# Splitting the preparation of a bias block's x into two parts in an attention and mixture-of-experts kernel

## The chip, the cores and the metric

The kernel runs on one core of one Trainium2 chip. The metric is the device time of one execution in microseconds; lower is better. Five engines work side by side, each through its own list of instructions in order, and meet through semaphores: PE (TensorE, matmuls), DVE (VectorE), ACT (ScalarE), POOL (GpSimd) and SP, which issues most DMAs.

## The reference

Attention with a learned position bias, then a dense layer pair, then a mixture of experts. The change touches the bias alone:

```python
def _attn_ref(q, k, v, w1, b1, w2):          # B, H, S, D = 4, 8, 576, 64
    scores = scale * np.matmul(q, k.transpose(0, 1, 3, 2))
    rel = (pos[:, None] - pos[None, :])
    psi_rel = np.log1p(np.abs(rel)); psi_i = np.log1p(np.maximum(pos[:, None], 1.0))
    x = (psi_rel / psi_i)[..., None]          # 576 x 576 x 1
    h = np.maximum(x @ w1 + b1, 0.0)          # w1: 1 x 32
    bias = h @ w2                             # w2: 32 x 8, one plane for each head
    scores = scores + bias.transpose(2, 0, 1)[None]
    ...                                       # softmax, times v
# then moe: (clip(h + 3, 0, 6) * h / 6) @ w_out, then moe2: 8 experts, top 1 of 8 by a gate
```

## The kernel before, in words

The whole program is written out as straight code by Python, and each engine runs its instructions in the order in which the code emits them.

The 576 query rows are cut into five chunks (`CH`): chunk 0 has 64 rows, chunks 1 to 4 have 128. The bias of a chunk is made in 9 blocks of 64 key columns, so there are 45 blocks; the text numbers them 0 to 44, and blocks 9, 18, 27 and 36 are the first of chunks 1 to 4. A block goes through these steps:

- `bias_load` gives the block its tiles of x, in turn out of five buffers (xb0 to xb3 and cv), and loads them by SP. In chunk 0 a block has one tile. In chunks 1 to 4 it has two of 128 x 1024 numbers, which this document calls its first and its second **half**.
- `bias_h` makes max(w1 x + b1, 0) in each half, one instruction per half. The table `KIND` says where: kind T on DVE out of a table (L231), kind D on DVE in place (L224), kind A on ACT in place (L221).
- `bias_mm` multiplies by w2 on PE into the PSUM tile pb (L240): the first half feeds column groups 0 and 1 of the array, the second half groups 2 and 3. Then pb is evicted to the SBUF tile bt (L246 and L249 on ACT, L253 on DVE).
- `bias_tr` transposes bt on PE into pbt (L263), and two instructions evict pbt into the bias planes: on ACT for kinds A and T (L273, L277), on DVE for kind D (L277).

In `emit`, `step_m(i)` is the first three for block i, and a lambda of `bias_tr` the last. The list `bq` orders them as m(0), m(1), t(0), m(2), t(1), m(3), ...; at a chunk's end it is m(8), t(7), t(8), m(9), m(10), t(9), and so on. `bh(i)` prepares every block up to i that is not prepared yet, and `step_m(i)` calls `bh(i + 1)` ahead of its own products. The steps are dealt out, 18 for each chunk, over the 36 places marked B in the string `ORDER0`, between the attention of the first three units (six items s for each chunk):

```python
ORDER0 = "Q0 T0 X0 B Q1 X1 B S T1 B P B B B N"
```

Q is a pair's scores (sc, L324 on PE) and the reading of them with the bias by DVE (L327); X the exponentials (L335, ACT); N the norm (L341, L342 on DVE, L344 on POOL); T the transposes of an item three steps back (pt, L362 on PE, evicted to eT by L366 on ACT and L368 on DVE); P its product with v (po, L378 and L382 on PE, evicted by L386 on ACT). pb, pbt, pt and po take their PSUM banks in turn from four (m0 to m3), so each waits until the tile four allocations before it has been evicted.

The stage with these blocks lies at about 10 to 172 us of the profiled execution. Attention of the other units follows, then the dense layers, then the experts.

Of the kernel before, what the change touches and what calls it, by code (L numbers as in the profile page):

```python
# [157 lines left out]
class Attn(Base):  # L158
# [48 lines left out]
            ts.append(x)  # L207
        return ts

    def bias_h(self, c, blk, ts):  # L210
        nc = self.nc
        r0, R = CH[c]
        kind = KIND[c][blk]
        nt = R // 64
        if kind == "T" and not self.lib[c][1]:
            lb = self.lib[c][0]
            nc.vector.tensor_scalar(lb[:, 1, :], lb[:, 0, :], self.nb1, None, op0=ALU.mult)
            self.lib[c][1] = True
        for t, x in enumerate(ts):
            if kind == "A":  # L220
                nc.scalar.activation(x, x, AF.Relu, bias=self.b1c, scale=self.w1c)  # L221
            elif kind == "D":

                nc.vector.tensor_scalar(x, x, self.w1c, self.nb1, op0=ALU.mult, op1=ALU.max)  # L224
            else:

                ncg = 4 // nt
                o = blk * 64 + t * ncg * 4 - r0 + 575
                v = self.tab[:, 0:1]
                view = bass.AP(tensor=v.tensor, offset=v.offset + o, ap=[v.ap[0], [4, ncg], [16, 4], [-1, R]])  # L230
                nc.vector.tensor_tensor(x, view, self.lib[c][0][:, 1:2, :].rearrange("p (a o) r -> p a o r", o=1).to_broadcast([P, ncg, 4, R]), op=ALU.max)  # L231
# [158 lines left out]
    def emit(self, extra):  # L390

        items = []
        for gi, g in enumerate(GROUPS):
            for c in range(len(CH)):
                for u in g:
                    for pr in range(2):
                        items.append((gi, c, u, pr))
        n0 = 2 * len(GROUPS[0])
        uc = []
        for it in items:  # L400
            if (it[2], it[1]) not in uc:
                uc.append((it[2], it[1]))
        first = {}
        for s, it in enumerate(items):
            first.setdefault(it[2], s)
        N = len(items)

        seq_b = [(c, blk) for c in range(len(CH)) for blk in range(9)]
        M = len(seq_b)
        loads, bts = {}, {}  # L410
        bq = []

        ldone, hdone = [0], [0]

        def bl(i):
            while ldone[0] <= min(i, M - 1):
                loads[ldone[0]] = self.bias_load(*seq_b[ldone[0]])
                ldone[0] += 1

        def bh(i):  # L420
            while hdone[0] <= min(i, M - 1):
                self.bias_h(*seq_b[hdone[0]], loads[hdone[0]])
                hdone[0] += 1


        def step_m(i):
            bh(max(i + 1, min(i + 2, 8)))
            bts[i] = self.bias_mm(*seq_b[i], loads.pop(i))
            bl(max(i + 3, min(i + 5, 8)))

        for i in range(M + 1):
            if i < M:
                bq.append((i - 1, lambda i=i: step_m(i)))
            if i > 0:
                bq.insert(len(bq) - (i % 9 == 0 and i < M), (i - 1 - (i % 9 == 0), lambda i=i: self.bias_tr(*seq_b[i - 1], bts.pop(i - 1))))
        bdone = [0]

        def bstep(n, upto=M):
            while n > 0 and bdone[0] < len(bq) and bq[bdone[0]][0] < upto:
                bq[bdone[0]][1]()  # L440
                bdone[0] += 1
                n -= 1

        qs = {}

        def q_load(i):
            if i < len(uc):
                qs[uc[i]] = self.load_q(*uc[i])


        self.setup()
        bl(4)
        for u in range(3):
            self.zero_v(u)
        self.load_k(0)
        q_load(0)
        bh(1)
        bstep(2, 9)
        q_load(1)
        bstep(6, 9)  # L460
        self.load_v(0)
        self.load_k(1)
        q_load(2)
        bstep(99, 9)


        side = [[] for _ in range(N + 4)]
        for i in range(1, len(uc)):
            s0 = next(s for s, it in enumerate(items) if (it[2], it[1]) == uc[i])
            side[max(0, s0 - 1)].append(lambda i=i: q_load(i + 2))  # L470
        side[0].insert(0, lambda: (self.load_v(1), self.load_k(2)))
        side[3].append(lambda: self.load_v(2))
        for u in range(3, 8):
            side[first[u] - (3 if u == 3 else 9)].append(lambda u=u: self.load_k(u))
            side[first[u] - (0 if u == 3 else 4)].append(lambda u=u: self.load_v(u))
        for s, fs in extra.items():
            side[s].extend(fs)

        es, eTs = {}, {}
        for s in range(N + 4):  # L480
            g0 = s < N and items[s][0] == 0
            upto = 9 * (items[s][1] + 2) if g0 else M
            slot = [0]

            def nb():
                if g0:
                    slot[0] += 1
                    want = 18 + 18 * (s * 6 + slot[0]) // (6 * n0)
                    bstep(max(0, want - bdone[0]), upto)

            if g0 and s % n0 == 0:
                bstep(99, 9 * (items[s][1] + 1))
            a = items[s] if s < N else None
            b = items[s - 1] if 0 <= s - 1 < N else None
            c = items[s - 3] if 0 <= s - 3 < N else None
            d = items[s - 4] if 0 <= s - 4 < N else None
            if a:
                es[s] = self.new_e(s)
            for k in (ORDER0 if g0 else ORDER).split():
                if k[0] == "Q" and a:  # L500
                    self.qk(*a[1:], int(k[1]), qs[(a[2], a[1])], es[s])
                elif k[0] == "X" and b:
                    self.sm_exp(*b[1:], es[s - 1], int(k[1]))
                elif k == "N" and b:
                    self.sm_norm(*b[1:], es[s - 1])
                elif k[0] == "T" and c:
                    if k == "T0":
                        eTs[s - 3] = self.new_eT(s, c[1])
                    self.pv_tr(*c[1:], es[s - 3], eTs[s - 3], int(k[1]))
                elif k == "P" and d:  # L510
                    self.pv(s, *d[1:], eTs.pop(s - 4))
                elif k == "S":
                    for f in side[s]:
                        f()
                elif k == "B":
                    nb()
# [872 lines left out]
```

## Time and profile before

| | |
|---|---|
| median of 3 runs | 1071.23 us (1069.64 to 1074.22) |
| profiled execution | 1073.36 us, span on the core 1071.6 us |
| mean granted TensorE clock | 0.986 |
| PE busy | 1014.0 us, 95% of the span |
| DVE busy | 620.8 us, 58% |
| ACT busy | 539.5 us, 50% |
| POOL busy | 220.6 us, 21% |

"Busy" is time in which an engine has an instruction in work. For matmuls the ends are modelled, and they overlap, so a stretch in which PE is 90% busy can still hold it up at every wait. The span runs from the first to the last instruction; the rest of the execution's time lies around it. The shares are means over stages with different limits.

### The profile page before, as it was taken

How to read it: one execution, taken by the hardware profiler on the slowest of the kernel's cores; microseconds unless marked ns; L12 is line 12 of the kernel's file. 1: busy time of each engine (PE TensorE's matmuls, PEld its weight loads, DVE VectorE, ACT ScalarE, POOL GpSimd, SP SyncE). 2: the span in 40 equal slices, each digit the busy share in tenths (PEclk: the TensorE clock that was granted, in tenths of full speed). 3: DMA queues.
4: the chain of work that ended last, by engine and by line, in shares of the span. 5: the costliest groups of instructions: out<-in, count | busy, mean ns of one | idle time of the engine just before them, and what ended most of it. 6: DMA issues, size and time to landing. Idle time of an engine off the chain costs nothing. (4 is left out here: it accounts for less than half of the span.)

```text
span 1071.6 us, 22490 instructions
## 1 busy us (share of the span) xinstructions
PE 1014.0 (95%) x8373; PEld 799.7 (75%) x8373; DVE 620.8 (58%) x1578; ACT 539.5 (50%) x1222; POOL 220.6 (21%) x273
## 2 busy tenths in 40 slices
PE   5898999989999989999999999999999989999996
PEld 2355556767777779988888889888887868777774
DVE  4886886768887767775445343436464633355310
ACT  4677788767778745554333333333352233354421
POOL 0132233534454200000010000002212242221111
PEclk9999999989999989999999999999999989999998
DMA  7564582423234134440202011010502185786850
GB/s 243 177 195 154 176 270 75 116 75 100 78 101 119 58 120 128 127 135 3 72 9 40 1 40 41 1 40 1 201 17 50 53 272 189 270 288 259 329 171 32
DMA packets 62198, 129.29 MB, mean 121 GB/s; under 512 B 13820, under 2 KB 35708, under 8 KB 59264
## 3 DMA queue, kind: packets, MB, share of 16 engines
q1 hardware_dynamic: 57424, 117.69, 33.3%
q0 software_dynamic: 4512, 9.49, 3.0%
q8 instruction: 68, 1.11, 0.4%
q10 hardware_dynamic: 144, 0.59, 0.2%
q14 instruction: 50, 0.41, 0.1%
HBM read 164.08 MB, written 14.65 MB: 167 GB/s over the span
## 5 line engine op out<-in xcount | busy, mean ns | idle before, releaser
L709 PE MATMUL acc<-wp,g 128*128 128x512 f32 x864 | 225.3, 396 | 0.7 <-DVE t L686 0.6
L679 PE MATMUL ph<-xh,wp 128*128 128x256 f32 x1024 | 207.0, 285 | 2.5 <-DVE eT L368 1.3
L679 PEld LDWEIGHTS ph<-xh,wp 128*128 128x128 f32 x1024 | 166.3, 189 | 12.2 <-issue 3.9
L709 PEld LDWEIGHTS acc<-wp,g 128*128 128x128 f32 x864 | 153.1, 189 | 27.5 <-DVE t L686 1.2
L344 POOL TENSOR_SCALAR e<-e,st 128x576 f32<-128x576 f32 (+1 forms) x160 | 126.2, 800 | 229.5 <-DVE st L342 109.2
L679 PE MATMUL ph<-xl,wp 128*128 128x256 f32 x512 | 144.2, 282 | 0.4 <-issue 0.4
L327 DVE CUSTOM_DVE_ANT_0 e<-sc,bias 128x576 f32<-128x576 f32 (+1 forms) x160 | 116.0, 752 | 46.4 <-PE sc L324 42.6
L685 ACT ACTIVATE r<-ph,small 128x256 f32<-128x256 f32 x144 | 67.5, 468 | 124.1 <-PE ph L679 119.0
L335 ACT ACTIVATE e<-e,st 128x576 f32<-128x576 f32 (+1 forms) x160 | 123.0, 774 | 0.0
L686 DVE SCALAR_TENSOR_TENSOR t<-r,ph 128x256 f32<-128x256 f32 x144 | 60.3, 419 | 107.8 <-ACT r L685 98.8
L688 ACT ACTIVATE g<-t 128x256 fp32r<-128x256 f32 x144 | 60.2, 418 | 114.2 <-DVE t L686 113.2
L1032 PE MATMUL peh<-ws,xt 128*128 128x512 f32 x408 | 102.8, 406 | 4.1 <-PEq L1341 4.0
L324 PE MATMUL sc<-K,q 64*128 64x288 f32 (+1 forms) x640 | 104.6, 426 | 0.4 <-DVE st L327 0.4
L679 PEld LDWEIGHTS ph<-xl,wp 128*128 128x128 f32 x512 | 96.7, 189 | 3.4
L783 POOL DMA_INDIRECT tab_d<-small x18 | 18.2, 1009 | 380.1 <-DVE small L781 343.0
L691 DVE SCALAR_TENSOR_TENSOR g<-t,g 128x256 fp32r<-128x256 f32 x144 | 61.0, 424 | 56.2 <-ACT g L688 55.7
L1032 PEld LDWEIGHTS peh<-ws,xt 128*128 128x128 f32 x408 | 76.9, 192 | 22.2 <-issue 4.9
L378 PE MATMUL po<-eT,V 128*64 128x128 f32 (+1 forms) x1280 | 82.2, 271 | 4.2 <-ACT eT L366 2.4
L1060 PE MATMUL peo<-ws,ehh 128*128 128x512 f32 x272 | 86.2, 398 | 0.0
L362 PEld LDWEIGHTS pt<-cst,e 64*128 64x128 f32 x1296 | 60.3, 139 | 34.5 <-issue 10.4
L378 PEld LDWEIGHTS po<-eT,V 128*64 128x64 f32 x1280 | 64.3, 138 | 27.4 <-issue 14.7
L362 PE MATMUL pt<-cst,e 64*128 64x64 f32 x1296 | 72.6, 232 | 8.6 <-ACT eT L366 3.5
(215 smaller groups left out, 1453.4 us busy)
## 6 DMA issues: line engine op xcount, KB each, us to landing
er<-in_we SPq DMA_DIRECT2D x46, 1024.0 KB
er<-in_we SPq DMA_DIRECT2D x86, 512.0 KB
xb<-in_xb SPq DMA_DIRECT2D x38, 512.0 KB
wraw<-in_wf SPq DMA_DIRECT2D x32, 512.0 KB
cv<-in_xb SPq DMA_DIRECT2D x11, 512.0 KB
K<-in_kT SPq DMA_DIRECT2D x8, 576.0 KB
xr<-xT_d SPq DMA_DIRECT2D x9, 512.0 KB
y_d<-y SPq DMA_DIRECT2D x18, 256.0 KB
```

Source lines behind the costliest of these rows:

```text
L324: nc.tensor.matmul(self.sc[i][:R, n, :288], q[d, pr, :], self.kv[u][d, pr, n * 288:(n + 1) * 288], start=True, stop=True, tile_position=(6 ...
L327: nc.vector.tensor_tensor_reduce(out=e[:R, j, :].rearrange("p (n s) -> p n s", n=2), in0=self.sc[j][:R, :, :288], in1=self.bias[c][:R, 4 * ...
L335: self.nc.scalar.activation(e[:R, j, :], e[:R, j, :], AF.Exp, scale=-1.0, bias=st[:R, j:j + 1], accum_out=st[:R, 4 + j:5 + j])
L344: nc.gpsimd.tensor_scalar(e[:R, j, :], e[:R, j, :], st[:R, 6 + j:7 + j], 1.0, op0=ALU.mult, op1=ALU.mult)
L362: nc.tensor.transpose(pts[h][:, i - a, :], src[i][d], self.ident[d, d], tile_position=(64 * h, 0))
L378: nc.tensor.matmul(po[64 * j:64 * j + 64, :], vm[:, 2 * pr + j, kb, :], eT[:, 2 * kb + j, :], start=kb == 0, stop=False, tile_position=(0, ...
L679: nc.tensor.matmul(ph, w, x[c], start=n == 0, stop=n == 11)
L685: nc.scalar.activation(r, ph, AF.Relu, bias=self.three)
L691: nc.vector.scalar_tensor_tensor(g[:, 1], t, 1.0 / 6.0, g[:, 0].bitcast(F32), op0=ALU.mult, op1=ALU.subtract)
L709: nc.tensor.matmul(acc[t], x, w, start=f == 0 and i == 0, stop=f == 15 and i == 2)
L1032: nc.tensor.matmul(ph[:, n, :], a, w, start=c == 0 and i == 0, stop=c == 3 and i == 2)
L1060: nc.tensor.matmul(d["po"], a, w, start=f == 0 and i == 0, stop=f == 7 and i == 2)
```

## The change

`bias_h` prepares one half per call. `bh` counts halves. `step_m(i)` makes sure that block i is whole, prepares the first half of block i + 1 and then issues the products of block i. The second half of block i + 2 is prepared by `step_t(i)`, behind the transposes of block i and their evictions. At the end of a chunk (`i % 9 == 8`) `step_t` prepares nothing, so the second half of the second block of the next chunk (blocks 10, 19, 28, 37) is made in its own `step_m`, directly ahead of its products. Blocks of chunk 0 have one tile, so nothing moves there.

```diff
-    def bias_h(self, c, blk, ts):
+    def bias_h(self, c, blk, ts, part):
...
-        for t, x in enumerate(ts):
+        for t, x in list(enumerate(ts))[part:part + 1]:
...
-        ldone, hdone = [0], [0]
+        ldone, hdone = [0], [0, 0]
...
-        def bh(i):
-            while hdone[0] <= min(i, M - 1):
-                self.bias_h(*seq_b[hdone[0]], loads[hdone[0]])
-                hdone[0] += 1
+        def bh(i, whole=True):
+
+            i = min(i, M - 1)
+            while hdone[0] < i or hdone[0] == i and (whole or hdone[1] == 0):
+                k, part = hdone
+                self.bias_h(*seq_b[k], loads[k], part)
+                hdone[:] = [k, part + 1] if part + 1 < len(loads[k]) else [k + 1, 0]
 
 
         def step_m(i):
-            bh(max(i + 1, min(i + 2, 8)))
+            bh(max(i, min(i + 2, 8)))
+            bh(i + 1, False)
             bts[i] = self.bias_mm(*seq_b[i], loads.pop(i))
             bl(max(i + 3, min(i + 5, 8)))
+
+        def step_t(i):
+            self.bias_tr(*seq_b[i], bts.pop(i))
+            if i % 9 < 8:
+                bh(i + 2)
...
-                bq.insert(len(bq) - (i % 9 == 0 and i < M), (i - 1 - (i % 9 == 0), lambda i=i: self.bias_tr(*seq_b[i - 1], bts.pop(i - 1))))
+                bq.insert(len(bq) - (i % 9 == 0 and i < M), (i - 1 - (i % 9 == 0), lambda i=i: step_t(i - 1)))
```

The lists of PE and SP hold the same instructions in the same order as before. On DVE and ACT the same instructions stand in another order. Three places show how.

DVE at the start of chunk 1 before: xb_52 and xb_53 are the two halves of block 10, ISA is the reading of the scores sc of the first item, xb_57 and cv are block 11's halves, and bt_71 evicts block 10's products.

```order
L231 TENSOR_TENSOR xb_52_239<-tab_73,lib_46_219 128x1024
L231 TENSOR_TENSOR xb_53_240<-tab_73,lib_46_219 128x1024
L327 ISA e_285,st_66_286<-sc_287,bias_134 64x576
L327 ISA st_66_286 64x1
L327 ISA e_285,st_66_286<-sc_288,bias_134 64x576
L327 ISA st_66_286 64x1
L231 TENSOR_TENSOR xb_57_257<-tab_73,lib_46_219 128x1024
L231 TENSOR_TENSOR cv_258<-tab_73,lib_46_219 128x1024
L253 SCALAR_TENSOR_TENSOR bt_71_307<-lib_46_219,nb_1_70,pb_302 128x512
```

The same place in the changed kernel:

```order
L231 TENSOR_TENSOR xb_52_239<-tab_73,lib_46_219 128x1024
L327 ISA e_284,st_66_285<-sc_286,bias_134 64x576
L327 ISA st_66_285 64x1
L327 ISA e_284,st_66_285<-sc_287,bias_134 64x576
L327 ISA st_66_285 64x1
L231 TENSOR_TENSOR xb_53_240<-tab_73,lib_46_219 128x1024
L231 TENSOR_TENSOR xb_57_256<-tab_73,lib_46_219 128x1024
L253 SCALAR_TENSOR_TENSOR bt_71_306<-lib_46_219,nb_1_70,pb_301 128x512
L231 TENSOR_TENSOR cv_257<-tab_73,lib_46_219 128x1024
```

Block 10's second half has moved from ahead of the readings to behind them, and block 11's from ahead of the eviction bt_71 to behind it.

DVE in chunk 2 before, where xb_163 and xb_164 are the halves of block 22, `bias` <- `pbt` evicts the transposes of block 20 and bt_196 the products of block 22:

```order
L231 TENSOR_TENSOR xb_163_683<-tab_73,lib_115_471 128x1024
L231 TENSOR_TENSOR xb_164_684<-tab_73,lib_115_471 128x1024
L341 TENSOR_SCALAR st_153_636<-st_153_636 128x2
L342 RECIPROCAL st_153_636<-st_153_636 128x2
L327 ISA e_775,st_186_776<-sc_777,bias_313 128x576
L327 ISA e_775,st_186_776<-sc_778,bias_313 128x576
L277 COPY bias_685<-pbt_795 128x4x64 x2
L368 COPY eT_189_784<-pt_802 128x256
L253 SCALAR_TENSOR_TENSOR bt_196_828<-lib_115_471,nb_1_70,pb_823 128x512
```

The same place in the changed kernel:

```order
L231 TENSOR_TENSOR xb_163_682<-tab_73,lib_115_470 128x1024
L341 TENSOR_SCALAR st_153_635<-st_153_635 128x2
L342 RECIPROCAL st_153_635<-st_153_635 128x2
L327 ISA e_774,st_186_775<-sc_776,bias_312 128x576
L327 ISA e_774,st_186_775<-sc_777,bias_312 128x576
L277 COPY bias_684<-pbt_794 128x4x64 x2
L231 TENSOR_TENSOR xb_164_683<-tab_73,lib_115_470 128x1024
L368 COPY eT_189_783<-pt_802 128x256
L253 SCALAR_TENSOR_TENSOR bt_196_827<-lib_115_470,nb_1_70,pb_822 128x512
```

The second half has moved behind the readings of one item's scores and behind the eviction of block 20's transposes, ahead of the eviction eT.

ACT a little later, where cv and xb_184 are the halves of block 24, bt_208 evicts block 23's products and `bias` <- `pbt` block 22's transposes, before and then changed:

```order
L221 ACTIVATE cv_767<-cv_767,cst 128x1024
L221 ACTIVATE xb_184_769<-xb_184_769,cst 128x1024
L246 COPY bt_208_877<-pb_872 128x512
L366 COPY eT_204_852<-pt_883 128x4x64
L386 COPY xo_194_819<-po_895 128x64
L273 ACTIVATE bias_685<-pbt_908,cst 128x4x64 x2
```

```order
L221 ACTIVATE cv_766<-cv_766,cst 128x1024
L246 COPY bt_208_876<-pb_871 128x512
L366 COPY eT_204_852<-pt_882 128x4x64
L386 COPY xo_194_819<-po_894 128x64
L273 ACTIVATE bias_684<-pbt_907,cst 128x4x64 x2
L221 ACTIVATE xb_184_768<-xb_184_768,cst 128x1024
```

Here three evictions and bt_208 have come ahead of the second half.

## Rows read from the trace of the kernel before

**Rows 1.** Busy time by stretch: us, each engine, PEclk, DMA share, GB/s.

```profile
20.00:172.00 152.00, 136.98 (x1414) 76.86 (x1414) 115.69 (x261) 118.29 (x268) 38.28 (x46) 0.99 0.58 192
...
32.00:36.00 4.00, 2.31 (x14) 0.69 (x12) 4.00 (x8) 2.19 (x7) 0.00 (x0) 1.00 0.57 217
...
80.00:84.00 4.00, 2.25 (x12) 0.92 (x12) 1.46 (x4) 2.90 (x7) 1.46 (x2) 0.67 0.09 21
```

**Rows 2.** PE's waits from 18 to 175 us: total, times, longest.

```profile
PE pbt L263 <- ACT bt L246: 3.1, 3, 2.7
...
PE pbt L263 <- ACT eT L366: 1.4, 1, 1.4
PE pbt L263 <- DVE bt L253: 1.2, 1, 1.2
PE po L378 <- DVE eT L368: 1.1, 1, 1.1
...
PE pt L362 <- ACT bt L249: 0.7, 1, 0.7
```

**Rows 3.** Groups of instructions by form, 20 to 172 us: count, busy, mean ns.

```profile
L231 DVE TENSOR_TENSOR xb<-tab,lib 128x1024 f32<-128x1024 f32 x23 | 28.2, 1258 | 0.1
L327 DVE CUSTOM_DVE_ANT_0 e<-sc,bias 128x576 f32<-128x576 f32 x37 | 27.6, 753 | 15.9 <-PE sc L324 15.5
...
L221 ACT ACTIVATE xb<-xb,cst 128x1024 f32<-128x1024 f32 x20 | 24.4, 1245 | 1.0 <-DMA xb<-in_xb 0.9
...
L224 DVE TENSOR_SCALAR xb<-xb,cst,nb 128x1024 f32<-128x1024 f32 x15 | 11.9, 813 | 3.0 <-DMA xb<-in_xb 3.0
...
L273 ACT ACTIVATE bias<-pbt,cst 128x256 f32<-128x256 f32 x26 | 10.8, 472 | 6.5 <-PE pbt L263 6.5
...
L277 DVE COPY bias<-pbt 128x256 f32<-128x256 f32 x18 | 6.8, 416 | 4.8 <-PE pbt L263 4.8
```

**Rows 4.** Timeline at the start of chunk 1: start, us, instructions, idle before.

```profile
23.90 2.36 DVE L231 TENSOR_TENSOR xb<-tab,lib 128x1024 f32<-128x1024 f32 x2
...
27.56 1.19 PE L324 MATMUL sc<-K,q 64*64 64x288 f32 x8
...
28.68 1.07 PE L240 MATMUL pb<-xb,w2b 128*32 128x512 f32 x8
28.89 0.75 DVE L327 CUSTOM_DVE_ANT_0 e<-sc,bias 64x576 f32<-64x576 f32 x1 [2.63 <-PE sc L324]
...
30.26 1.21 DVE L231 TENSOR_TENSOR xb<-tab,lib 128x1024 f32<-128x1024 f32 x1
...
32.66 1.05 PE L240 MATMUL pb<-cv,w2b 128*32 128x512 f32 x4
...
35.90 2.10 PE L240 MATMUL pb<-xb,w2b 128*32 128x512 f32 x8 [1.60 <-DVE xb L231]
```

**Rows 5.** Timeline at the start of chunk 2, then around block 22.

```profile
60.09 1.24 PE L324 MATMUL sc<-K,q 64*128 64x288 f32 x8
...
62.54 0.62 PE L240 MATMUL pb<-cv,w2b 128*32 128x512 f32 x2
...
72.10 0.66 PE L263 MATMUL pbt<-cst,bt 128*128 128x128 f32 x4
...
73.10 0.75 DVE L327 CUSTOM_DVE_ANT_0 e<-sc,bias 128x576 f32<-128x576 f32 x1
...
73.78 0.75 DVE L277 COPY bias<-pbt 128x256 f32<-128x256 f32 x2
73.80 0.16 PEld L240 LDWEIGHTS pb<-xb,w2b 128*32 128x32 f32 x8
```

**Rows 6.** Timeline around block 24.

```profile
80.00 1.23 ACT L221 ACTIVATE xb<-xb,cst 128x1024 f32<-128x1024 f32 x1
81.13 0.56 ACT L246 COPY bt<-pb 128x512 f32<-128x512 f32 x1
...
81.75 1.11 PE L263 MATMUL pbt<-cst,bt 128*128 128x128 f32 x4 [2.69 <-ACT bt L246]
```

## The prediction

> **What bounds the kernel now.** The change touches only the stage with the bias blocks, so I read that stage first, in the view of busy time by stretch [rows 1]. From 20 to 172 us PE is busy for 137 of 152 us, ACT for 118 and DVE for 116. No engine is full, so the waits between them decide, and PE is the one to watch: it has about 15 us of idle time here, and whatever it loses nobody gives back, because every later stage starts behind it and runs on PE again. Second, PE's waits [rows 2]. The longest are not for x. They are for evictions: 2.7 us for one bt on ACT, 1.4 for an eT on ACT, 1.2 for a bt and 1.1 for an eT on DVE, 0.7 for a bt on ACT. Rows 6 show how the longest came about: bt could not start before 81.13 because the second half of block 24's x stood ahead of it on ACT (80.00, 1.23 us), and PE sat for 2.69 us. That is what the change can win. Third, the durations [rows 3]: a half costs 1.26 us as kind T, 1.25 as A and 0.81 as D; a reading of scores 0.75; an eviction of transposes 0.47 on ACT and 0.42 on DVE, and each block has two. Last, the timeline at places where the order changes [rows 4 to 6]: what the reader is to see is how long before its product a half is ready today.
>
> **The change part by part.** Nothing is added or removed. PE and SP keep their order, so the question at each block is only when its second half is ready against when PE comes to its product, and which evictions come earlier in exchange. There are 36 blocks with two halves.
>
> Chunk starts (blocks 10, 19, 28, 37). Today DVE makes both halves of block 10 from 23.90 to 26.26 and then idles for 2.63 us until the scores come [rows 4]. PE runs the products at 28.68 in one go, 1.07 us for all four column groups. In the changed order the second half waits behind both readings, which start at 28.89 and free DVE at 30.26; 1.21 us later it is ready, at about 31.5. The products of half a block take 1.05 us alone [rows 4], as long as those of a whole one, so they end at about 32.65 instead of 29.75: 2.9 us. Block 9's second half, behind two evictions on ACT, adds some 0.6, which makes 3.5. Some of this was lost before anyway, since PE waited 1.60 us at 35.90 for DVE's pair of halves; DVE itself will be about 2 us late there, so I let 0.7 come back and take 2.8. At chunk 2, scores start at 60.09 and the product at 62.54 [rows 5]. Readings end 2.7 us after the scores start (28.89 - 27.56 + 1.37, rows 4), one eviction of eT of about 0.4 follows, then 1.26 for the half: 64.5 or so, against 62.54, 2.0 late. For block 28 (kind D, 0.81, with about 0.9 more of PE's work between) the same steps give 0.6, for block 37 (kind T) 1.5. Sum 6.9.
>
> Second halves that now stand behind the eviction of block i - 2's transposes on the same engine. By the table KIND these are 12: 14, 15, 16, 18, 22, 24, 27, 29, 30, 31, 42, 43. For six of them (15, 18, 24, 27, 30, 42) PE's next work after those transposes is the product itself. From the start of the transposes it takes 0.66 us for them [rows 5], some 0.8 for two evictions, then 1.25 or 0.81 for the half, so PE finds the second half up to 2.0 us late (1.6 for D). Where today's pair is late as well, the loss is smaller; at the best placed of the six I find 0.75. I take 1.3 each: 7.8. At the other six there are transposes of pt or a product po between. Block 22 is such a place: DVE evicts at 73.78 for 0.75, then the half needs 1.26, so its products start at about 75.8 instead of 73.80 [rows 5], less 0.4 because the readings come sooner without the pair ahead of them: 1.6. For the other five I take 0.4 each, between nothing and 1.2. Sum 3.6.
>
> Three more second halves (13, 26, 33) fall behind a reading or an eviction without the transposes' chain: one half of D's length each, 2.4 together. The remaining 16 are hidden behind scores, pt and po; uncovered, each would cost up to its 1.25.
>
> What is won: evictions that stood behind a pair. In rows 2, the 2.7 shrinks by the one half that leaves (81.13 - 80.00 = 1.1), the 1.4 almost wholly (1.3), of the 1.2 half (0.6), the 1.1 and the 0.7 wholly. Sum 4.8, with a lower bound of 2 (if a lag on PE lets these waits vanish anyway, they are won once and not twice) and an upper of 7.5, all five rows.
>
> The clock. Granted clock is 1.00 in 32 to 36 us although PE waits there [rows 1], and 0.67 in 80 to 84 us, where PE had idled for 2.69 us; the transposes at 81.75 take 1.11 us [rows 6] instead of 0.66 [rows 5]. At half speed for these microseconds PE lost about 1.3 us, and the shorter wait may save that. The Trainium skill, "TensorE: Matmul & The Clock Gate", section "A second HAM failure mode: psum-queue depth-cycling", goes against this change: it says that PE idling often and briefly between groups of matmuls is enough for the clock to go back and forth between its levels. From 20 to 172 us this trace shows a mean of 0.99 [rows 1], which is the one fall. By the rows the clock is worth -1.3; by the page, with PE in short waits at every second block, it would be a loss. I count neither in the sum.
>
> Sum: 6.9 + 7.8 + 3.6 + 2.4 - 4.8 = 15.9 us. The profiled execution took 1073.4 us (span 1071.6), 2.1 above the median of the runs but within them; added to the median of 1071.2 this is 1087. The bounds: everything at its lowest (chunk starts 4, the six adjacent at 0.75, nothing else) and all 7.5 won gives +1, about 1072; everything at its highest (6.9 + 12 + 7.6 + 2.4, 2 won) gives +27, about 1098.
>
> **The rivals.**
> - The engines catch up. Once PE is 5 us behind, DVE and ACT, which idle for about 35 us each in this stage, run ahead, and later second halves are ready after all. Then the chunk starts and few adjacent places stay: 6.9 + 3 - 4.8, about +5, 1076. For it speaks that idle time; against it that each eviction waits for PE's own transposes, so the chain starts anew at each block however free DVE is.
> - Earlier evictions win. If a second half is in time at nearly every block, what is left is the 7.5 us of rows 2 and the clock's 1.3: 1062. It needs PE's waits for second halves to stay below about 8.8 / 36 = 0.25 us per block. Rows 2 speak for it; against it, at six blocks PE has nothing to do between transposes and product.
> - The clock falls repeatedly. PE at about 82% busy instead of 90%, with a wait of 1 to 2 us at every second block. Five more falls at 1.3 us: 1087 + 6.5, about 1093. For it: the fall at 81 us. Against: 32 to 36 us, where PE was busy for only 2.31 of 4 us at full clock.
> - Nothing: losses and gains of this size cancel, 1071.
>
> **How the numbers follow.** The forecast as summed 0.55, the clock 0.18, catching up 0.14, earlier evictions 0.07, nothing 0.06. A difference of 0.5%, some 5.4 us, is about what a measurement of this kernel tells from no change. Slower by more than that: the forecast, the clock and a third of catching up: 0.78. Within: the rest of catching up, and nothing: 0.15. Faster: 0.07. The range from 1074 to 1096 leaves out the earlier evictions and the ends of the bounds.
>
> **What would show it.** In the profile after, PE and SP have the same counts, and DVE's and ACT's busy times stay. The last transposes of the stage, today at 170, start at about 186. PE's idle time ahead of L240, released by L231, L221 and L224, grows from a few us to more than 15, most of it at the listed blocks and chunk starts; each such product splits into two groups of about 1.05 us. The wait of 2.69 us shrinks to about 1.6 and the fall of the clock behind it goes. From 190 us on, the timeline is the same, shifted. The prediction is wrong if second halves are ready when PE comes, so that the idle time ahead of L240 hardly grows, or if the stage loses time through waits for scores or evictions instead.

## The result and the profile after

| | before | changed |
|---|---|---|
| median of the runs, same chip | 1071.58 us (1069.64 to 1074.22) | 1088.18 us (1086.61 to 1090.88) |
| profiled execution, span | 1073.36 us, 1071.6 us | 1086.61 us, 1084.8 us |
| mean granted clock over the span | 0.986 | 0.989 |
| start of the stage's last transposes | 169.31 us | 186.14 us |

The changed kernel is slower: 1.0137 times the time of before, 95% interval 1.0111 to 1.0164, or 16.6 us by the medians. In a second set it was 1.0131 (1.0103 to 1.0158).

First the busy time by stretch of the changed kernel (columns as in [rows 1]).

```profile
20.00:172.00 152.00, 135.01 (x1253) 69.27 (x1246) 107.14 (x237) 105.74 (x239) 32.51 (x40) 0.99 0.56 179
32.00:36.00 4.00, 4.00 (x18) 1.51 (x20) 2.89 (x4) 2.16 (x6) 0.00 (x0) 0.57 0.41 131
80.00:84.00 4.00, 3.65 (x43) 2.21 (x39) 3.19 (x8) 3.17 (x8) 1.48 (x2) 1.00 0.80 211
88.00:92.00 4.00, 2.45 (x40) 1.55 (x36) 2.61 (x7) 3.64 (x10) 1.79 (x3) 1.00 0.03 10
```

In the same 152 us PE issues 1253 matmuls instead of 1414, though it is busy for nearly as long (137 us before). Next its waits from 18 to 188 us (total, times, longest).

```profile
PE pb L240 <- DVE xb L231: 7.0, 8, 1.8
PE pb L240 <- ACT xb L221: 3.3, 4, 1.1
PE pbt L263 <- ACT bt L246: 2.3, 3, 1.6
PE pb L240 <- DVE xb L224: 1.8, 2, 1.2
PE pb L240 <- ACT cv L221: 1.0, 1, 1.0
```

Four of the five longest are now for halves of x, 13.1 us together where the kernel before has 3.3. All but 0.9 us of it is for second halves (block 12, made on DVE from 36.70 us, waits 0.87 for its first). The wait for block 23's bt, 2.69 us in [rows 6], has shrunk to 1.6. The last view is that of the groups by form, here from 20 to 186 us.

```profile
L240 PE MATMUL pb<-xb,w2b 128*32 128x512 f32 x228 | 51.7, 607 | 13.1 <-DVE xb L231 7.0 <-ACT xb L221 3.3 <-DVE xb L224 1.8
L231 DVE TENSOR_TENSOR xb<-tab,lib 128x1024 f32<-128x1024 f32 x23 | 27.7, 1216 | 0.1
...
L221 ACT ACTIVATE xb<-xb,cst 128x1024 f32<-128x1024 f32 x20 | 24.6, 1247 | 0.5 <-DMA xb<-in_xb 0.4
```

The kernel before has this row for the products from 20 to 172 us:

```profile
L240 PE MATMUL pb<-xb,w2b 128*32 128x512 f32 x228 | 42.6, 612 | 3.6 <-DVE xb L231 1.8 <-ACT bias L277 0.9 <-DVE eT L368 0.3
```

The halves take the durations of [rows 3]; what grows is PE's idle time ahead of these products, from 3.6 to 13.1 us whatever it waits for. (That 13.1 stands in the view above too is chance: there it is the waits for x ahead of all products.) The busy time of the products grows too, from 42.6 to 51.7, because two groups of two column groups, issued apart, take about 1.05 us each.

How much is idle time and how much is busy time shows in PE's share of the stage up to the start of its last transposes, in the kernel before and then in the changed kernel's second profile (after_again, below):

```profile
20.00:169.31 149.31, 134.29 (x1380) 74.58 (x1380) 115.44 (x260) 116.70 (x262) 36.88 (x45) 0.99 0.59 194
20.00:184.66 164.66, 145.81 (x1377) 76.04 (x1373) 114.40 (x259) 117.04 (x260) 35.39 (x45) 1.00 0.55 177
```

Of the 15.4 us by which the stage grows PE is busy for 11.5 and idle for 3.8. A part of each wait for a second half is covered by the first half's product, which occupies PE for as long as a whole one; and the longer waits for halves are partly paid for by shorter ones for evictions (PE's idle time ahead of the transposes of 128 rows falls from 6.4 to 2.1 us).

At the start of chunk 1 the timeline of the changed kernel shows the cut:

```profile
28.43 1.05 PE L240 MATMUL pb<-xb,w2b 128*32 128x512 f32 x4
...
30.01 2.35 DVE L231 TENSOR_TENSOR xb<-tab,lib 128x1024 f32<-128x1024 f32 x2
31.27 1.05 PE L240 MATMUL pb<-xb,w2b 128*32 128x512 f32 x4 [1.79 <-DVE xb L231]
...
32.37 0.75 DVE L253 SCALAR_TENSOR_TENSOR bt<-lib,nb,pb 128x512 f32<-128x512 f32 x1
...
33.13 2.19 PE L324 MATMUL sc<-K,q 64*64 64x288 f32 x8
...
38.06 1.05 PE L240 MATMUL pb<-xb,w2b 128*32 128x512 f32 x4 [0.87 <-DVE xb L231]
```

Block 10's first half goes through PE at 28.43. For its second half PE waits 1.79 us, and this product ends 2.6 us later than that of [rows 4]. Then the eviction bt starts at 32.37. In the kernel before it started at 32.53, since there DVE made block 11's two halves between the readings and bt (30.26 to 32.53), and here block 10's second and block 11's first (30.01 to 32.37): the same work, so against the kernel before the late product costs almost nothing at this place. It takes away what bt would have won without block 11's second half ahead of it: in e1 (below) it starts 1.2 us sooner. The last row is block 12's first half.

That is how I read all blocks: by the start of bt in the timelines of DVE and ACT, that is the moment when a whole product is there and its engine is free. The "step" is what the lag against the kernel before grows by at a block. The changed kernel's second profile is used, whose clock did not fall in this stage. Every step over 0.5 us that raises the lag, and every one over 0.6 that lowers it:

```
block   bt before   bt changed   step      block   bt before   bt changed   step
 9        27.85       28.05     +0.64       26        93.59      103.64     +0.72
12        38.92       40.31     +0.91       28       104.35      113.60     -0.67
13        42.73       45.22     +1.10       29       107.28      117.70     +1.17
14        45.85       49.49     +1.15       30       110.16      122.44     +1.86
15        47.37       52.99     +1.98       31       115.42      128.71     +1.01
16        52.53       59.30     +1.15       32       120.37      132.99     -0.67
18        60.30       67.45     +0.60       37       139.76      153.82     +1.30
19        64.64       72.75     +0.96       40       153.33      165.89     -1.86
20        67.60       76.69     +0.98       41       155.83      169.66     +1.27
21        70.74       78.98     -0.85       43       166.03      180.25     +0.84
22        75.03       84.72     +1.45       44       168.55      183.90     +1.13
23        81.13       89.72     -1.10
24        84.79       94.15     +0.77
```

The lag goes from -0.44 at block 8 to +15.35 at block 44. A step need not lie at the block that caused it: where bt stood behind its engine's other work in the kernel before, a late product moves bt only at a later block. Block 19's product ends 9.10 us later than before (72.70 for 63.61 us) and block 20's as well (75.76 for 66.66), so by the ends of the products block 19 has a step of 1.91 and block 20 one of 0.00, where bt divides it into 0.96 and 0.98: in the kernel before, block 19's bt started at 64.64, 1.0 us behind its product. Single steps are therefore to be read together with their neighbours, and with the experiments.

From block 12 on the two profiles of the changed kernel agree in nearly all steps to within 0.03 us (39, 41 and 42 differ by 0.2 to 0.5); the largest difference is at block 11, +0.01 against +1.19, behind the fall of the clock at 32 to 36 us in the first of them.

### The profile page after: what moved, and what is told of

Its sections match the earlier page's. It is cut to its first block, busy times and chain, and to the rows that moved or that the text cites. A ratio compares the mean times of both kernels' runs of the same rounds, so it can differ in the third digit from the quotient of the medians.

```text
span 1084.8 us, 22490 instructions
## 1 busy us (share of the span) xinstructions
PE 1023.9 (94%) x8373; PEld 798.8 (74%) x8373; DVE 620.7 (57%) x1578; ACT 541.4 (50%) x1222; POOL 219.9 (20%) x273
## 3 DMA queue, kind: packets, MB, share of 16 engines
q8 instruction: 69, 1.13, 0.4%
## 5 line engine op out<-in xcount | busy, mean ns | idle before, releaser
L688 PEld LDWEIGHTS ph<-xh,wp 128*128 128x128 f32 x1024 | 166.1, 188 | 11.5 <-issue 3.3
L362 PEld LDWEIGHTS pt<-cst,e 64*128 64x128 f32 x1296 | 60.1, 139 | 32.8 <-issue 10.2
L378 PEld LDWEIGHTS po<-eT,V 128*64 128x64 f32 x1280 | 64.2, 138 | 26.6 <-issue 15.9
```

Of the source, the lines that this page charges most:

```text
L362: nc.tensor.transpose(pts[h][:, i - a, :], src[i][d], self.ident[d, d], tile_position=(64 * h, 0))
L378: nc.tensor.matmul(po[64 * j:64 * j + 64, :], vm[:, 2 * pr + j, kb, :], eT[:, 2 * kb + j, :], start=kb == 0, stop=False, tile_position=(0, ...
L688: nc.tensor.matmul(ph, w, x[c], start=n == 0, stop=n == 11)
```

## The experiments

All kernels with the times by ratio to the kernel before on the same chip, since the chips differ (its medians in the four sets were 1071.6, 1076.1, 1074.3 and 1075.2 us). The times that the expectations name are on the scale of the first set. The last column is the start of the stage's last transposes in the profiled execution.

| | ratio, 95% interval | last transposes at |
|---|---|---|
| before | 1 | 169.31 |
| changed | 1.0137 (1.0111 to 1.0164) | 186.14 |
| after_again | 1.0131 (1.0103 to 1.0158) | 184.66 |
| e1_starts_whole | 1.0074 (1.0057 to 1.0091) | 181.02 |
| e2_half_ahead_of_tr | 1.0071 (1.0045 to 1.0098) | 178.05 |
| e3_both | 1.0033 (1.0016 to 1.0049) | 174.03 |
| e4_behind_bt | 0.9959 (0.9940 to 0.9979) | 171.01 |
| e4_again | 0.9997 (0.9976 to 1.0017) | 171.40 |
| e5_late_first | 1.0217 (1.0189 to 1.0244) | 200.78 |
| e6_adjacent_whole | 1.0095 (1.0068 to 1.0122) | 179.84 |
| e7_separated_whole | 1.0068 (1.0043 to 1.0094) | 181.18 |
| e8_pair_behind_bt | 1.0018 (0.9998 to 1.0038) | 176.45 |
| e9_before_late_first | 1.0021 (1.0002 to 1.0041) | 174.29 |

The stage's end is the sharper reading of the two. From there to the end of the span the 13 profiles take 898.7 to 905.2 us, whatever the stage did; the instructions are the same, and part of the difference is the clock in later stages. For the changed kernel and the one before:

```profile
core 0: 1084.8 us, clock 0.989
core 0: 1071.6 us, clock 0.986
```

Span times (1 - clock) is 1084.8 x 0.011 = 11.9 us here and 1071.6 x 0.014 = 15.0 in the kernel before, and the difference of 3.1 us is most of what lies between the span's growth, 13.2, and the stage's, 16.8. A single execution can be off the stage by some 3 us for such reasons.

**after_again**, the changed kernel once more, beside e5 to e7. 

> The changed kernel itself, beside the other kernels of this set, so that they are compared on one chip. Expected by every theory: 1.0137 times the kernel before, within 1.011 to 1.017.

Measured 1.0131, as expected. Below, "gives back" is against its 184.66. (By block 8, ahead of anything that changes, the kernels already differ from it by up to 0.8 us; where it matters, the figure counted from there is given too.)

**e1_starts_whole.** The second block of a chunk gets both halves ahead of the products of the block in front.

```diff
-            bh(i + 1, False)
+            bh(i + 1, i % 9 == 0)
```

> The changed kernel, but at the chunk starts both halves of blocks 10, 19, 28 and 37 are made ahead of block 9's, 18's, 27's and 36's products, as before. If second halves that are late cost what PE's timeline shows at these blocks (2.8, 1.9, 1.0 and 1.4 us), the time falls by about 7 us from 1088 to 1081, and PE's waits for x at these four products go. If later waits absorb what is saved (the stage has a length of its own, whatever its start), it falls by 2 us or less.

The stage ends 3.6 us earlier (4.0 counted from block 8); by the times it is some 6 (0.006 of 1071). By the steps of bt it gives back 1.0 at blocks 9 and 10, 1.2 at 19 to 21, 0.4 at 28 and 1.4 at 37. The chunk starts cost, but little over half of the 7 us that was expected. By the ends of the products one sees why: with both halves in time, the products of blocks 10, 19, 28 and 37 end 2.83, 1.91, 1.00 and 1.41 us sooner, as long as was expected, but 1.59, 0.72 and 0.57 of it go again at blocks 11, 21 and 29.

**e2_half_ahead_of_tr.** The second half goes ahead of the transposes' evictions instead of behind them.

```diff
         def step_t(i):
-            self.bias_tr(*seq_b[i], bts.pop(i))
             if i % 9 < 8:
                 bh(i + 2)
+            self.bias_tr(*seq_b[i], bts.pop(i))
```

> The changed kernel, but the second half of block i + 2 is made ahead of block i's transposes and their evictions, not behind them; the chunk starts stay as in the change. If the chain transposes, evictions, half, product is what costs at the 12 blocks where evictions and half share an engine (6.9 us at the six where PE comes to the product at once, 5.0 at the six others), most of it goes: 1088 - 9 = 1079. If the loss comes from the half standing behind the readings of scores, whatever the transposes do, less than 3 us come back: 1085 or more.

The stage ends 6.6 us earlier (6.9 from block 8), and the ratio falls by as much: most of the 9 that were expected, and more than the rival's 3. The steps lie at blocks 15 (0.8), 16 (0.5), 18 (0.5), 22 (0.7), 24 (1.2), 27 (0.7), 30 (1.0) and 42 to 43 (0.8): all of them blocks whose second half shares its engine with these evictions; of the 12 such blocks 14, 29 and 31 give nothing back. Its waits from 18 to 180 us show what is late in their place:

```profile
PE pb L240 <- DVE xb L231: 5.2, 7, 1.8
PE pb L240 <- ACT bias L277: 3.2, 4, 1.4
```

Now the evictions stand behind a half, and products wait 3.2 us in all, in four waits, for the bank of an earlier pbt (0.9 in the row of the kernel before above).

**e3_both**, e1 and e2 together. 

> Both edits together: chunk starts whole, and elsewhere the second half ahead of the transposes. If the two losses add, 1088 - 7 - 9 = 1072, within 3 us of the kernel before, and the evictions that come earlier stay won. If they overlap (one lag hides the other), 1077 or more.

10.6 us of the stage come back, against 3.6 + 6.6 = 10.2 for the two apart (from block 8 it is 11.4 against 10.9), so they are separate losses. What stays, 4.7 us of the stage and 1.0033, some 3.5 us by the times, lies a little outside the 3 us of the expectation and short of its rival; no run takes this rest apart.

**e6_adjacent_whole** and **e7_separated_whole** undo the change at six blocks each.

```diff
-            bh(i + 1, False)
+            bh(i + 1, i + 1 in (15, 18, 24, 27, 30, 42))
```

> The changed kernel, but at the six blocks 15, 18, 24, 27, 30 and 42 the second half stands ahead of the product of the block in front again. Theory: these cost 6.9 us by the lags in the two traces (7.8 by the prediction), and the longer wait for block 23's evicted product comes back for about 1.1 and others for up to 1, so 5 to 6 us less than the changed kernel, a ratio of 1.008 to 1.009 to the kernel before. Rival, that the following block takes up the lateness whichever block it begins at: 2 us or less come back, 1.012 or more.

> The changed kernel, but at the six blocks 14, 16, 22, 29, 31 and 43 the second half stands ahead of the product of the block in front again. Theory: these cost 5.0 us by the lags in the two traces (3.6 by the prediction), less up to 1.5 of evictions that come later again, so 3 to 5 us less than the changed kernel, a ratio of 1.009 to 1.011. Rival, that PE's other work between a block's transposes and the next product covers them and the lag seen there was passed on from the blocks in front: 1 us or less, 1.013.

(e7 has 14, 16, 22, 29, 31 and 43 in the list.) e6 gives back 4.8 us of the stage (5.5 from block 8) and e7 3.5; e7's clock fell within 32 to 38 us, which cost 1.2 at block 11, so 4.7 without that. The ratios fall by 0.0036 and 0.0063, less and more than expected, and the stage by about what was expected in both. So the lateness does belong to the place: the six blocks with PE's work in between cost as much as the six without it. e6 also shows the wins going back. Its timeline for PE at block 23's transposes and its busy time by stretch:

```profile
89.81 0.66 PE L263 MATMUL pbt<-cst,bt 128*128 128x128 f32 x4 [2.69 <-ACT bt L246]
```

```profile
88.00:92.00 4.00, 2.19 (x18) 1.08 (x20) 0.39 (x3) 3.44 (x8) 1.46 (x2) 1.00 0.10 18
```

With block 24's second half ahead of bt again, the 2.69 us of [rows 6] are back to the last digit. But the transposes behind it take 0.66 us, at full clock, where they took 1.11 in the kernel before.

**e5_late_first.** The last two column groups first, so that no product is cut any more.

```diff
-        for cg in range(4):
+        for cg in (2, 3, 0, 1):
```

> The changed kernel, with the four column groups of a block's product issued in the order 2, 3, 0, 1, so that the second half is used first. Theory that the time is lost between the second half and the end of the product: half a product took 1.05 us and a whole one 1.07, so the product ends as long behind the second half as before, and the time stays that of the changed kernel within 2 us. Rival, that cutting a product in two groups costs PE time in itself: no product is cut any more, about 25 places of up to 1.0 us, so 10 us or more come back.

Both expectations failed: it is slower than the changed kernel by 0.0086, some 9 us, and in the profiled execution, the slowest of its four, its stage ends 16.1 later than after_again's. The busy time by stretch of e5 in the two parts of the stage:

```profile
20.00:112.00 92.00, 67.98 (x524) 32.34 (x526) 51.84 (x109) 49.99 (x111) 14.23 (x18) 0.80 0.42 142
112.00:202.00 90.00, 75.54 (x872) 46.91 (x870) 62.98 (x152) 68.49 (x155) 21.39 (x28) 1.00 0.56 179
```

and that of after_again in the first part:

```profile
20.00:112.00 92.00, 77.38 (x674) 37.00 (x670) 62.88 (x133) 60.79 (x137) 18.15 (x22) 1.00 0.53 173
```

The timeline of e5 for PE early in the stage and in chunk 4:

```profile
33.62 1.93 PE L240 MATMUL pb<-xb,w2b 128*32 128x512 f32 x8 [2.87 <-DVE xb L231]
35.48 1.12 PE L263 MATMUL pbt<-cst,bt 128*128 128x128 f32 x4
...
42.45 1.06 PE L240 MATMUL pb<-xb,w2b 128*32 128x512 f32 x8 [2.96 <-DVE xb L231]
43.45 1.90 PE L324 MATMUL sc<-K,q 64*64 64x288 f32 x8
...
168.69 1.06 PE L240 MATMUL pb<-xb,w2b 128*32 128x512 f32 x8 [1.45 <-DVE xb L231]
169.68 0.66 PE L263 MATMUL pbt<-cst,bt 128*128 128x128 f32 x4
```

Without a half product in between, PE idles in one piece, 2.9 us instead of 1.79 at block 10, and in this part of the stage the granted clock drops again and again to the lower of its two levels (1.2 GHz instead of 2.4): the whole product at 33.62 takes 1.93 us, the one at 42.45 still 1.06, and the scores behind it 1.90. The mean of 0.80 over 92 us is 92 x 0.20 = 18 us of clock withheld, which costs time only while PE has work. By bt, e5 lags after_again by 14.9 us at block 26, and by 16.1 at block 44: from 112 us on, where the clock holds at 1.00, the order of the groups costs almost nothing, as the theory had it. So the theory is borne out where the clock is the same. What it left out is the clock: with the first half's product issued early, PE's idle time comes in shorter pieces, and after_again's clock was 1.00 in the same stage. That the length of the pieces is the reason is argued and not shown: e5 waits 2.07 us for block 30's second half, at 136.43 us, and the clock stays at 1.00.

**e9_before_late_first**, the same edit in the kernel before, as the control. 

> The kernel before, with the four column groups of a block's product issued in the order 2, 3, 0, 1. A control for e5_late_first. Theory: the order costs nothing by itself, since both halves are ready together, so 0.998 to 1.003 of the kernel before, and the 10 us that e5_late_first lost against the changed kernel belong to the longer waits and the clock. Rival: the order itself costs, 1.008 or more.

1.0021 (1.0002 to 1.0041): within the expectation, hardly more than nothing. Its stage ends 5.0 us later, with the largest steps at blocks 13 (1.4, at a fall of the clock) and 42 (1.5). The order is not quite free in a kernel where some pairs come late, but that is far from e5's 16 us.

**e4_behind_bt.** The second half is moved to the other side of the product: right behind bt of the block in front, on every engine.

```diff
         def step_m(i):
             bh(max(i, min(i + 2, 8)))
             bh(i + 1, False)
             bts[i] = self.bias_mm(*seq_b[i], loads.pop(i))
+            bh(i + 1)
             bl(max(i + 3, min(i + 5, 8)))
 
         def step_t(i):
             self.bias_tr(*seq_b[i], bts.pop(i))
-            if i % 9 < 8:
-                bh(i + 2)
```

> The second half of block i + 1 directly behind block i's products and their eviction bt, so it is later than before by one eviction (0.6 to 0.75 us) and not by a chain. If late second halves are the whole loss, it is gone, and the evictions bt that stood behind a pair keep what they won (1.1, 0.6 and 0.7 us): 1069, within 2 us. If cutting the pair in two costs by itself (products in two groups of column groups, a half at a time), it stays 3 us or more above the kernel before: 1075.

> The same kernel as e4_behind_bt, in more rounds and on another chip: the second half of a block's x stands right behind the evicted product (bt) of the block in front. Theory that it is faster than before because the waits for evicted products get shorter: 0.996 again, within 0.994 to 0.998. Rival: in the profiles its stage with the bias ends 1.7 us later than in the kernel before, so the gain comes only from where the clock falls in the later stages, and a second set gives 0.998 to 1.002.

The first set gave 0.9959, the second, with more rounds, 0.9997: the rival of the second expectation, not the theory. In the profiles its stage ends 1.7 and 2.1 us later than that of the kernel before; but the mean clock from 20 to 172 us was 0.98 and 0.97 in them, against 0.99 there, a difference of 1.5 to 3 us of clock, so even that lateness isn't shown to be the order's. I take it as no faster: 13 to 15 us of the stage are saved against the changed kernel, and no gain on the kernel before is shown. The waits of its first profile from 18 to 180 us have no half of x at their head:

```profile
PE po L378 <- DVE eT L368: 2.6, 2, 2.1
PE pbt L263 <- ACT bt L246: 1.9, 3, 1.6
PE pb L240 <- DVE xb L231: 1.6, 2, 0.9
```

The wait for bt is down to 1.6 as in the changed kernel, but a longer one for eT, 2.1 us, has come up. Its timeline for DVE and PE shows it:

```profile
148.17 0.81 DVE L224 TENSOR_SCALAR xb<-xb,cst,nb 128x1024 f32<-128x1024 f32 x1 [0.64 <-DMA xb<-in_xb]
...
149.89 0.48 DVE L368 COPY eT<-pt 128x320 f32<-128x320 f32 x1
...
150.43 0.87 PE L378 MATMUL po<-eT,V 128*64 128x128 f32 x8 [2.15 <-DVE eT L368]
```

The moved half waits on DVE for its load, and the norm, the reading and the eviction eT stand behind it. In the kernel before, that eT starts at 148.99 and the wait is the 1.1 us of [rows 2].

**e8_pair_behind_bt**, both halves behind bt of the block in front.

```diff
         def step_m(i):
             bh(max(i, min(i + 2, 8)))
-            bh(i + 1, False)
             bts[i] = self.bias_mm(*seq_b[i], loads.pop(i))
+            bh(i + 1)
```

> The kernel before in its structure, with no half apart: both halves of a block's x stand right behind the evicted product (bt) of the block in front, where the kernel before has them right ahead of it. Theory: bt no longer waits for the pair, which wins what the halves behind bt win in e4_behind_bt, but both halves are now made in the time between bt and the next product, so at the blocks where little of PE's work lies between (the six adjacent ones and the chunk starts) the pair is up to 1.25 us later than in e4_behind_bt: 1.002 to 1.008 of the kernel before. Rival: only the place behind bt matters and there is time for both, 0.995 to 0.999.

(The diff leaves out that the line in `step_t` goes, as in e4.) 1.0018 (0.9998 to 1.0038), at the lower end of the theory; the stage ends 7.1 us later than in the kernel before. In that profile the mean clock from 20 to 172 us was 0.96, a deficit of 152 x 0.04 = 6 us against 1.5 in the kernel before, so the clock alone could make most of the 7.1. Whether there is less slack for two halves than for one is not shown by this profile; by the ratios e8 lies 0.2% above e4's second set, within the intervals.

## Why the prediction was right

**The mechanism.** PE now waits for second halves: 13.1 us for halves of x where there were 3.3, and the stage ends 16.8 us later (15.4 in after_again, 15.9 predicted). e1, e2, e6 and e7 each take the cause away at the places named and get time back there. The time came out at 1088.2 for 1087. This is less idle time than the "more than 15" that was written down, and PE did not fall to 82% busy but stayed at 89%: the products cut in two, which the prediction had seen at block 10, take up a part of each wait. The busy times of DVE and ACT stayed (620.7 and 541.4 us), and the last transposes start at 186.14 where about 186 was written down.

**The terms** fit less well than their sum. By the steps of bt in after_again:
- Chunk starts: 6.9 predicted; e1 gives back 3.6. The lateness of the four products was right (2.83, 1.91, 1.00 and 1.41 us by e1, for 2.9, 2.0, 0.6 and 1.5). The step that failed is "so I let 0.7 come back", and that nothing was let come back at blocks 19 and 28: blocks 9 to 11 cost 0.9 and not 2.8, because DVE makes two halves between the readings and bt in either order, and bt was as late before. Block 37 was right (1.3 for 1.5), at block 19 the 2.0 were there (1.91 by the ends of the products), and 0.7 came back at block 21, so e1 gives back 1.2 there, and at block 28 e1 gives back 0.4 for 0.6.
- Six adjacent blocks: 7.8 predicted. Their steps sum to 4.6 (15: 1.98, 18: 0.60, 24: 0.77, 27: -0.13, 30: 1.86, 42: -0.45), and e6 gives back 4.8. The 1.3 each was too much for 18, where today's pair was late as well, a case that the prediction had named, and for 27, where PE waits only 0.49 us for the half. At 42 bt was late in the kernel before by its engine, 2.07 us behind its product; e6 gives back 0.9 at 42 and 43.
- Six separated blocks: 3.6 predicted, and here the size was off the other way. The steps sum to 6.8; e7 gives back 4.7. Block 22 was right (1.45 for 1.6). The other five came to 0.8 to 1.2 each by the steps, the upper end of "between nothing and 1.2", and to some 0.65 each by e7, where 0.4 was taken. The work between transposes and product does not wholly cover the half.
- Blocks 13, 26 and 33: 2.4 predicted, 1.10 + 0.72 + 0.41 = 2.2 measured.
- The 16 that were called hidden: by the steps of bt four were not, 12, 20, 41 and 44, with 0.91, 0.98, 1.27 and 1.13. By the ends of the products these four have no step (-0.01, 0.00, -0.10 and 0.00), and the lateness is that of blocks in front, as at 19 and 20 above. So they may well have been hidden.
- Won: 4.8 predicted. The steps down sum to 5.8: 17 (0.22), 21 (0.85), 23 (1.10), 28 and 32 (0.67 each), 36 (0.41), 40 (1.86). Block 23's 1.10 is the 1.1 that was read from [rows 6]. Not all of it is evictions: 0.7 at block 21 is what comes back of block 19's lateness, since e1 has no such step.

So by the steps of bt the chunk starts and adjacent blocks were put some 6 to 7 us too high, and the separated and hidden ones as much too low. By the ends of the products the terms lie nearer: 7.0 for blocks 9 to 11, 19, 28 and 37, 4.2 for the adjacent, 4.9 for the separated, 2.1 for 13, 26 and 33, and -2.5 for the 16 with what was won. Either way errors of 3 us and more cancel, and that the sum came within 1 us is luck.

**The rivals.** That the engines catch up is refuted as an account of the whole, since the lag grows from 9.9 us at block 27 to 15.4 at block 44; on a small scale it is what gives 2.9 us back behind three of the chunk starts. That earlier evictions win is refuted in size: 5.8 won against more than 20 lost. That the clock falls repeatedly did not happen in the changed kernel: the mean from 20 to 172 us is 0.99, one fall in one profile and none in the other. But e5 shows how near it was. The Trainium skill, "TensorE: Matmul & The Clock Gate", section "A second HAM failure mode: psum-queue depth-cycling", tells of a bf16 kernel whose clock goes back and forth because PE idles often and briefly between groups of matmuls. e5 agrees with that, with 0.80 over 92 us; the changed kernel doesn't, though it too waits for halves at 14 of the 36 blocks, in shorter pieces of up to 1.8 us.

**The clock's place.** The 1.3 us that the prediction left out of its sum, the fall behind the 2.69 us wait, did go: 88 to 92 us, where that wait is now 1.55, is at 1.00. That the shorter wait is the reason is not shown, since e6 has the whole wait and no fall. In the first profile another came at 32 to 36 us (0.57).

## What to carry to other kernels

When an operation is moved back in an in-order queue, read for each place what stands between its new position and its consumer, and whether the engine that consumes it was bound by the same queue anyway: a product 2.8 us late cost 1 us where the eviction behind it was already as late (blocks 9 to 11), and a late half some 0.8 us on average (e7) at places with work in between that looked like cover. A half that leaves one eviction's way stands in another's, so look for the slot with the most slack (of those tried behind the old place, right behind bt, which came out even with it) and not only for the wait to be removed. Keep some matmul that can start early ahead of a late one: it does not end sooner, but here the clock held with it and fell without it.

## What the runs showed of the hardware

- A product of two column groups (x4) takes 1.05 us, a whole one of four (x8) 1.06, at full clock, so a product cut in two takes up PE for 2.10 us; at the lower clock the whole takes 1.93.
- The same wait of 2.69 us ahead of block 23's transposes was followed by a fall of the clock in the kernel before (1.11 us for the transposes, 0.67 over 80 to 84 us, [rows 1]) and by none in e6 (0.66 us, 1.00 over 88 to 92). The wait of block 10 (1.79 and 1.80 us) was followed by one in the changed kernel's first profile and in e7, and by none in after_again, e2 and e6. What decides it stays open; a single wait's length does not.
- From block 12 on, steps of the lag repeat between the two profiles of the changed kernel to within 0.03 us at nearly all blocks, while the rest of the program, with the same instructions, differs by up to 6.5 us between the 13 profiles.
